# Weight conversion in pairs of tiles, with pair buffers, in a fused attention and two-layer kernel

## The chip, the cores and the metric

The kernel runs on one core of one Trainium2 chip. The metric is device time in microseconds (us) from start to end of one execution; several executions are timed and the median counts. A separate execution is taken by the hardware profiler, and its rows are what this document reads.

## What is computed

Attention with a learned relative bias, followed by two gated layers, all in fp32:

```python
scores = q @ k.T / sqrt(64) + bias(i, j)          # 4 batches, 8 heads, 576 x 576
x = softmax(scores) @ v                           # -> 2304 tokens x 512
x = (sigmoid(x @ w_gate) * (x @ w_val)) @ w_out   # 512 -> 1536 -> 512
h = x @ w_in                                      # 512 -> 2048
out = (h * clip(h + 3, 0, 6) / 6) @ w_out2        # -> 512
```

The five weight matrices come as 64-bit floats, which the host packs as they are, and are cut into 68 tiles of 128 x 512 numbers each, `wpack`, in the order of their use.

## The kernel before

**Blocks and steps.** The 576 query rows are cut into five chunks (`QC`): four of 128 and one of 64, which is 512 tokens, in the last 256, over the four batches. A *lead* stage computes the attention of chunk 0. Then come five blocks, `block(0)` to `block(4)`. Block k runs the 68 steps (`STEPS`, `NSTEP`) of the two layers on chunk k, one weight tile a step, and between the steps the attention and bias of chunk k + 1, placed by the list that `block_events` makes. So tile n mod 68 serves step n, and every tile is used five times.

**One step.** `product` multiplies with a weight tile that is split into a high half `wh` and a low half `wl`, so that fp32r matmuls (L613, L607) reach fp32: for each of four 128-row parts it runs `wh*xh`, `wh*xl`, `wl*xh`, twelve matmuls a step. In the last block the high and low half of x stand in one tile, and a step has eight or twelve shorter ones.

**The weights.** In block 0 the packed tiles are converted on the chip. `w_load` brings a raw tile `wd` (128 x 512 pairs of 32-bit words, 512 KB) from `wpack` (L531). `w_split` turns it into fp32 bits in the scratch tile `cm` and splits that: ScalarE scales the upper word (L575), VectorE shifts (L576), joins the lower word's upper bits (L577) and the sign (L580), ScalarE writes the high half (L585) and VectorE subtracts for the low half (L586). `w_store` writes the split tile `wp` to a buffer in HBM, `wsp` (L591). Blocks 1 to 4 only load split tiles from `wsp` (L535). Tiles 0 and 1 are converted in the lead by `w_part`, one operation at a time.

**Buffers and look-ahead.** There are six `wp` tiles, four raw tiles and two scratch tiles in block 0. At step n of block 0 the program issues the raw load of tile n + 6 (`WA + 1`), the store of tile n + 2 and the conversion of tile n + 3 (`WB`). From tile 68 on it issues at step n the load of tile n + 5 (`WA`).

**What sets the order.** In block 0 the instructions of TensorE and of the DMA queue SP run in the order of the program (`manual_schedule`), those of ScalarE and VectorE in an order that a planner makes at compile time. In blocks 1 to 4 only TensorE keeps the program's order; SP is planned too. Every engine then runs its instructions strictly in that fixed order. Waits come from the data: a write to a buffer waits for the last readers of the tile that had it before.

Of the kernel before, what the change touches and what calls it, by code (L numbers as in the profile page):

```python
# [30 lines left out]
SU = S + 31  # L31
WA = 5
WB = 3
# [25 lines left out]
def fused_kernel(ctx: ExitStack, tc: tile.TileContext, qd, kd, vd, tz, td, rd, zc, w2b, iden, wpack, out):  # L59
# [12 lines left out]
    z_p = pool("z", 2)  # L72
    w_p = pool("w", 6)

# [448 lines left out]

    wq, wf_q = {}, {}

    def w_load(n):
        if n >= NC * NSTEP:
            return
        if n < NSTEP:
            wd = A["wf"].tile([128, 512, 2], U32, name="wd")  # L530
            nc.sync.dma_start(out=wd.rearrange("p a b -> p (a b)"), in_=wpack[n].bitcast(U32))  # L531
            wf_q[n] = wd
        else:
            wp = w_p.tile([128, 2, 4, 128], F32R, name="wp")
            nc.sync.dma_start(out=wp.rearrange("p s c m -> p s (c m)").bitcast(F32), in_=wsp[n % NSTEP])  # L535
            wq[n] = wp

    cm_q = {}

    def w_part(n, part):  # L540

        if part == 0:
            cm_q[n] = A["cv"].tile([128, 512], U32, name="cm")
            wq[n] = w_p.tile([128, 2, 4, 128], F32R, name="wp")
        m = cm_q[n]
        f, wv = m.bitcast(F32), wq[n].rearrange("p s c m -> p s (c m)")
        low, high = wf_q[n][:, :, 0], wf_q[n][:, :, 1]
        if part == 0:
# [11 lines left out]
        elif part == 4:  # L560
            nc.vector.tensor_scalar(out=wv[:, 0], in0=f, scalar1=1.0, scalar2=None, op0=ALU.mult)
        else:
            nc.vector.tensor_tensor(out=wv[:, 1], in0=f, in1=wv[:, 0].bitcast(F32), op=ALU.subtract)
            nc.sync.dma_start(out=wsp[n], in_=wv.bitcast(F32))
            del wf_q[n], cm_q[n]

    def w_split(n):

        if n >= NSTEP:
            return  # L570
        wd = wf_q.pop(n)
        low, high = wd[:, :, 0], wd[:, :, 1]
        m = A["cv"].tile([128, 512], U32, name="cm")
        f = m.bitcast(F32)
        nc.scalar.activation(out=f, in_=high.bitcast(F32), func=AF.Copy, scale=2.0 ** -112)  # L575
# [6 lines left out]
        )  # L582
        wp = w_p.tile([128, 2, 4, 128], F32R, name="wp")
        wv = wp.rearrange("p s c m -> p s (c m)")
        nc.scalar.activation(out=wv[:, 0], in_=f, func=AF.Copy)  # L585
        nc.vector.tensor_tensor(out=wv[:, 1], in0=f, in1=wv[:, 0].bitcast(F32), op=ALU.subtract)  # L586
        wq[n] = wp

    def w_store(n):
        if 2 <= n < NSTEP:  # L590
            nc.sync.dma_start(out=wsp[n], in_=wq[n].rearrange("p s c m -> p s (c m)").bitcast(F32))  # L591

# [3 lines left out]
    def product(n, nt, ops, mm_ps, first=True, last=True, wide=False):  # L596
        wp = wq.pop(n)
        wh, wl = wp[:, 0], wp[:, 1]
        if first:
# [91 lines left out]
    with ExitStack() as lead:  # L691
        for name, bufs in (("pt", 2), ("s", 3), ("k", 6), ("v", 7), ("bo", 3), ("wf", 2), ("cv", 2)):
            A[name] = lead.enter_context(tc.tile_pool(name=name + "l", bufs=bufs))
# [63 lines left out]
    conv = ExitStack()  # L757
    for name, bufs in (("pt", 2), ("wf", 4), ("cv", 2)):
        A[name] = conv.enter_context(tc.tile_pool(name=name + "c", bufs=bufs, reuse_waits="tile"))
    ctx.enter_context(tc.issue_after(gate.ins))  # L760
    ctx.enter_context(tc.issue_after(gate_act.ins))
    for n in range(2, WA + 1):
        w_load(n)
# [133 lines left out]
    def block(k):  # L897
        ev = block_events(k)
        for i in range(NSTEP):
# [5 lines left out]
            if k == 0:  # L905
                if n + WA + 1 < NSTEP:
                    w_load(n + WA + 1)
                for x in range(WB - 1 if i == 0 else WB, WB + 1):
                    w_store(n + x - 1)
                    w_split(n + x)  # L910
            if n + WA >= NSTEP:
# [76 lines left out]
```

## Time and profile before

| what | value |
|---|---|
| three runs | 1104.69, 1105.45, 1105.76 us; median 1105.45 |
| profiled execution, its own time | 1102.25 us |
| its span, first to last instruction | 1100.2 us |
| granted TensorE clock | 1.000 of full speed (2.4 GHz) |
| lead; block 0; blocks 1 to 3; block 4 | about 0 to 84; 84 to 333; 333 to 999; 999 to 1097 us |
| busy: TensorE, VectorE, ScalarE, GpSimd | 99%, 62%, 49%, 12% of the span |

The stretches are those of the matmuls of line 613. PE is TensorE, PEld its weight load, DVE VectorE, ACT ScalarE, POOL GpSimd, SP the queue that issues most DMAs. Matmuls overlap each other and their ends are modelled. Operations of VectorE and ScalarE overlap by their ends as well, so that the distance from start to start is what one takes of the engine.

### The profile page before, as it was taken

Reading aid. Unit: us, or ns where it says so; the run is one execution under the profiler, and the core shown is the slowest. Engines: PE = TensorE matmul, PEld = TensorE weight load, DVE = VectorE, ACT = ScalarE, POOL = GpSimd, SP = SyncE. Lnnn points to the kernel's source line nnn. Section 1 sums busy time; section 2 is a strip of 40 time slices with the busy share of each in tenths; the row PEclk is TensorE's granted clock in tenths of the full one; section 3 lists DMA queues with packets and bytes.
Section 4 is the critical chain, followed back from the end, with each engine's and each line's share of the span. In section 5 each row is a group of like instructions: output and inputs, shape, how many; then the busy total and the mean of one; then the engine's idle time right before and its main releaser. Section 6 shows DMA issues by size and latency. Waiting matters only on the chain.

```text
span 1100.2 us, 19627 instructions
## 1 busy us (share of the span) xinstructions
PE 1088.0 (99%) x6964; PEld 873.7 (79%) x6964; DVE 679.8 (62%) x1571; ACT 534.7 (49%) x1087; POOL 129.9 (12%) x248
## 2 busy tenths in 40 slices
PE   8999999999999999999999999999999999999998
PEld 4777777777777787878778878788878888888898
DVE  8899998898972466887735654656352417153433
ACT  7887686798872534555424342444032214123332
POOL 2000000000010002121121111111440202031000
PEclk9999999999999999999999999999999999999999
DMA  7948999989986688999997888787996968678997
GB/s 235 369 179 296 376 396 374 387 322 370 392 291 235 212 278 288 283 318 287 308 320 249 288 248 276 263 264 248 287 289 212 286 225 280 212 242 309 370 371 272
DMA packets 118768, 321.96 MB, mean 293 GB/s; under 512 B 21008, under 2 KB 29712, under 8 KB 118672
## 3 DMA queue, kind: packets, MB, share of 16 engines
q1 hardware_dynamic: 108000, 297.15, 78.3%
q0 software_dynamic: 9152, 23.21, 7.5%
q8 instruction: 56, 0.92, 0.3%
q10 hardware_dynamic: 1520, 0.35, 0.2%
q14 instruction: 40, 0.33, 0.1%
HBM read 245.09 MB, written 51.37 MB: 269 GB/s over the span
## 4 chain that ended last, share of the span: by engine, by line
PE 82%; DVE 7%; ACT 4%; DMA 3%; issue 2%; SPq 1%; DVEq 0%; ACTq 0%
PE ps L613 61%; PE ps L430 7%; PE ps L607 6%; PE ps L477 2%; PE ps L386 2%; PE ps L335 2%; PE ps L171 1%; DVE cm L577 1%; DMA kt<-kd 1%; DVE wp L586 1%; DVE cm L580 1%; PE ps L483 1%; ACT cm L575 1%; DVE s L350 1%; DMA wd<-wpack 1%
## 5 line engine op out<-in xcount | busy, mean ns | idle before, releaser
L613 PE MATMUL ps<-xyh,wp 128*128 128x512 f32 (+1 forms) x1472 | 431.2, 379 | 0.2
L613 PEld LDWEIGHTS ps<-xyh,wp 128*128 128x128 f32 x1472 | 263.3, 188 | 58.1 <-DVE m L499 2.7
L613 PE MATMUL ps<-gh,wp 128*128 128x512 f32 (+1 forms) x980 | 298.9, 385 | 0.4 <-ACT gh L628 0.4
L613 PE MATMUL ps<-xyl,wp 128*128 128x512 f32 x640 | 249.7, 390 | 0.3 <-DVE xyl L632 0.3
L613 PEld LDWEIGHTS ps<-gh,wp 128*128 128x128 f32 x980 | 178.7, 188 | 37.7 <-issue 2.5
L613 PE MATMUL ps<-gl,wp 128*128 128x512 f32 x448 | 174.8, 390 | 0.2 <-DVE gl L630 0.2
L409 POOL DMA_DIRECT2D pT<-t x192 | 94.4, 500 | 495.1 <-DMA wp<-wsp 205.1
L628 ACT ACTIVATE gh<-tmp 128x512 fp32r<-128x512 f32 (+1 forms) x140 | 82.1, 587 | 127.5 <-DVE tmp L651 85.1
L613 PEld LDWEIGHTS ps<-xyl,wp 128*128 128x128 f32 x640 | 120.2, 188 | 24.9 <-DVE xyl L632 0.8
L360 ACT ACTIVATE s<-s,m 128x576 f32<-128x576 f32 x144 | 110.4, 769 | 23.8 <-DVE m L499 17.9
L630 DVE TENSOR_TENSOR gl<-tmp,gh 128x512 fp32r<-128x512 f32 x112 | 76.5, 685 | 35.7 <-ACT gh L628 34.8
L613 PEld LDWEIGHTS ps<-gl,wp 128*128 128x128 f32 x448 | 84.2, 188 | 17.1 <-DVE gl L630 0.7
L430 PEld LDWEIGHTS ps<-pT,vt 128*64 128x64 f32 x1600 | 79.3, 137 | 17.0 <-issue 11.6
L430 PE MATMUL ps<-pT,vt 128*64 128x128 f32 (+1 forms) x1600 | 92.1, 266 | 0.5 <-ACT pT L389 0.4
L657 DVE SCALAR_TENSOR_TENSOR tmp<-tmp,ps 128x512 f32<-128x512 f32 (+1 forms) x80 | 50.0, 628 | 55.2 <-ACT tmp L656 53.6
L651 DVE SCALAR_TENSOR_TENSOR tmp<-tmp,ps 128x512 f32<-128x512 f32 x48 | 32.7, 682 | 74.5 <-PE ps L613 73.8
L656 ACT ACTIVATE tmp<-ps 128x512 f32<-128x512 f32 (+1 forms) x80 | 43.9, 548 | 44.3 <-PE ps L613 44.0
L455 ACT ACTIVATE xyh<-ps 128x128 fp32r<-128x128 f32 (+1 forms) x52 | 16.4, 316 | 98.7 <-PE ps L430 98.5
L681 POOL DMA_DIRECT2D outT<-acc x40 | 27.7, 740 | 269.0 <-DVE acc L672 250.3
L399 DVE STREAM_TRANSPOSE t<-s 128x1152 f32<-128x1152 f32 x40 | 54.3, 1369 | 0.4
L373 DVE TENSOR_SCALAR s<-s,r 128x576 f32<-128x576 f32 x112 | 53.2, 517 | 1.4
L456 DVE TENSOR_TENSOR xyl<-ps,xyh 128x128 fp32r<-128x128 f32 (+1 forms) x48 | 16.0, 333 | 58.9 <-ACT xyh L455 58.6
(99 smaller groups left out, 1236.3 us busy)
## 6 DMA issues: line engine op xcount, KB each, us to landing
wp<-wsp SPq DMA_DIRECT2D x272, 512.0 KB, 5.1
wd<-wpack SPq DMA_DIRECT2D x68, 512.0 KB, 6.4
wsp<-wp SPq DMA_DIRECT2D x68, 512.0 KB, 6.0
vt<-vd SPq DMA_DIRECT2D x80, 320.0 KB, 5.0
kt<-kd SPq DMA_DIRECT2D x80, 288.0 KB, 5.3
pT<-t POOLq DMA_DIRECT2D x192, 72.0 KB, 4.9
pT<-t SPq DMA_DIRECT2D x128, 72.0 KB, 4.5
bm<-biasD SPq DMA_DIRECT2D x15, 576.0 KB, 6.4
```

What stands on the lines that cost most here:

```text
L360: nc.scalar.activation(out=s[:, h], in_=s[:, h], func=AF.Exp, scale=-1.0, bias=d["m"][:, h:h + 1], accum_out=r[:, h:h + 1],)
L373: nc.vector.tensor_scalar(out=s[:, h], in0=s[:, h], scalar1=r[:, h:h + 1], scalar2=None, op0=ALU.mult)
L399: nc.vector.transpose(out=tn_q[0][:, :, x], in_=st[u]["s"].rearrange("p h j -> p (h j)").rearrange("p (t q j) -> p q t j", q=4, j=32),)
L409: (nc.sync if p[0][0] < 4 and i > 1 else nc.gpsimd).dma_start(out=pt[32 * q:32 * q + 32, i].rearrange("j u t i -> j (u t i)"), in_=t[32 * ...
L430: nc.tensor.matmul(out=po[64 * h:64 * h + 64, n * a:n * a + n], lhsT=vt[:, v], rhs=pt[:, m * a:m * a + m, k, :], start=(t == 0), stop=(t = ...
L607: nc.tensor.matmul(out=o, lhsT=w[:, c, :], rhs=x, start=(first and c == 0 and w is wh), stop=(last and c == 3 and w is wh),)
L613: nc.tensor.matmul(out=ps[:, 0:nt], lhsT=w[:, c, :], rhs=x[:, 0:nt], start=(first and c == 0 and i == 0), stop=(last and c == 3 and i == 2),)
L628: nc.scalar.activation(out=hi, in_=src, func=AF.Copy, scale=scale)
L630: nc.vector.tensor_tensor(out=lo, in0=src, in1=hi.bitcast(F32), op=ALU.subtract)
L651: nc.vector.scalar_tensor_tensor(out=th, in0=th, scalar=1.0, in1=ps, op0=ALU.add, op1=ALU.mult)
L656: nc.scalar.activation(out=t, in_=ps, func=AF.Relu, bias=3.0)
L657: nc.vector.scalar_tensor_tensor(out=t, in0=t, scalar=6.0, in1=ps, op0=ALU.min, op1=ALU.mult)
```

## The change

Raw tiles, scratch and split tiles become pairs: `wp` has three buffers of two tiles each (the same memory as six), the raw tiles in block 0 three buffers of two (six tiles for four). From tile 4 on `w_split` runs each of its six operations once over two tiles, called at every second step for tiles n + 3 and n + 4; tiles 2 and 3 are done singly at step 0. The raw load of tile n + 7 (`WR`) is issued at step n, the store of tile n + 1 (for n + 2 before), and from tile 68 on the load of tile n + 4 (for n + 5). The scratch no longer has a pool of its own in block 0: up to tile 17 it takes a buffer of `pT`, then one of `z`.

```diff
--- before.py
+++ after.py
@@ -29,7 +29,8 @@
 NT = 320
 SW = S + NQ - 1
 SU = S + 31
-WA = 5
+WA = 4
+WR = 7
 WB = 3
 YG, OG = 3, 2
 BIG = 3.0e38
@@ -70,7 +71,7 @@
     st_p = pool("st", 4)
     bm_p = pool("bm", 2)
     z_p = pool("z", 2)
-    w_p = pool("w", 6)
+    w_p = pool("w", 3)
 
 
     s1 = pool("ps_s", 2, space=PS)
@@ -521,19 +522,28 @@
         att_x(p[0], po)
         del st[p[1]]
 
-    wq, wf_q = {}, {}
+    wq, wf_q, wp_q = {}, {}, {}
+
+    def w_tiles(n, k=1):
+
+        if n % 2 == 0:
+            wp_q[0] = w_p.tile([128, 2, 2, 512], F32R, name="wp")
+        for x in range(k):
+            wq[n + x] = wp_q[0][:, (n + x) % 2]
+        return wp_q[0][:, n % 2:n % 2 + k]
 
     def w_load(n):
         if n >= NC * NSTEP:
             return
         if n < NSTEP:
-            wd = A["wf"].tile([128, 512, 2], U32, name="wd")
-            nc.sync.dma_start(out=wd.rearrange("p a b -> p (a b)"), in_=wpack[n].bitcast(U32))
-            wf_q[n] = wd
+            if n % 2 == 0:
+                wf_q[0] = A["wf"].tile([128, 2, 512, 2], U32, name="wd")
+            nc.sync.dma_start(
+                out=wf_q[0][:, n % 2].rearrange("p a b -> p (a b)"), in_=wpack[n].bitcast(U32)
+            )
+            wf_q[1, n] = wf_q[0][:, n % 2:2]
         else:
-            wp = w_p.tile([128, 2, 4, 128], F32R, name="wp")
-            nc.sync.dma_start(out=wp.rearrange("p s c m -> p s (c m)").bitcast(F32), in_=wsp[n % NSTEP])
-            wq[n] = wp
+            nc.sync.dma_start(out=w_tiles(n)[:, 0].bitcast(F32), in_=wsp[n % NSTEP])
 
     cm_q = {}
 
@@ -541,10 +551,10 @@
 
         if part == 0:
             cm_q[n] = A["cv"].tile([128, 512], U32, name="cm")
-            wq[n] = w_p.tile([128, 2, 4, 128], F32R, name="wp")
+            w_tiles(n)
         m = cm_q[n]
-        f, wv = m.bitcast(F32), wq[n].rearrange("p s c m -> p s (c m)")
-        low, high = wf_q[n][:, :, 0], wf_q[n][:, :, 1]
+        f, wv, wd = m.bitcast(F32), wq[n], wf_q[1, n][:, 0]
+        low, high = wd[:, :, 0], wd[:, :, 1]
         if part == 0:
             nc.vector.tensor_scalar(out=f, in0=high.bitcast(F32), scalar1=2.0 ** -112, scalar2=None, op0=ALU.mult)
         elif part == 1:
@@ -562,16 +572,20 @@
         else:
             nc.vector.tensor_tensor(out=wv[:, 1], in0=f, in1=wv[:, 0].bitcast(F32), op=ALU.subtract)
             nc.sync.dma_start(out=wsp[n], in_=wv.bitcast(F32))
-            del wf_q[n], cm_q[n]
-
-    def w_split(n):
+            del cm_q[n]
+
+    def w_split(n, k=2):
 
         if n >= NSTEP:
             return
-        wd = wf_q.pop(n)
-        low, high = wd[:, :, 0], wd[:, :, 1]
-        m = A["cv"].tile([128, 512], U32, name="cm")
-        f = m.bitcast(F32)
+        wd = wf_q[1, n][:, 0:k]
+        low, high = wd[:, :, :, 0], wd[:, :, :, 1]
+        if n < 18:
+            m = A["pt"].tile([128, 9, NQ], F32, name="pT").rearrange("p t n -> p (t n)")
+        else:
+            m = z_p.tile([128, 4, S], F32, name="z").rearrange("p g j -> p (g j)")
+        f = m[:, 0:512 * k].rearrange("p (s a) -> p s a", s=k)
+        m = f.bitcast(U32)
         nc.scalar.activation(out=f, in_=high.bitcast(F32), func=AF.Copy, scale=2.0 ** -112)
         nc.vector.tensor_scalar(out=m, in0=m, scalar1=3, scalar2=None, op0=ALU.logical_shift_left)
         nc.vector.scalar_tensor_tensor(
@@ -580,22 +594,20 @@
         nc.vector.scalar_tensor_tensor(
             out=m, in0=high, scalar=0x80000000, in1=m, op0=ALU.bitwise_and, op1=ALU.bitwise_or
         )
-        wp = w_p.tile([128, 2, 4, 128], F32R, name="wp")
-        wv = wp.rearrange("p s c m -> p s (c m)")
-        nc.scalar.activation(out=wv[:, 0], in_=f, func=AF.Copy)
-        nc.vector.tensor_tensor(out=wv[:, 1], in0=f, in1=wv[:, 0].bitcast(F32), op=ALU.subtract)
-        wq[n] = wp
+        wv = w_tiles(n, k)
+        nc.scalar.activation(out=wv[:, :, 0], in_=f, func=AF.Copy)
+        nc.vector.tensor_tensor(out=wv[:, :, 1], in0=f, in1=wv[:, :, 0].bitcast(F32), op=ALU.subtract)
 
     def w_store(n):
         if 2 <= n < NSTEP:
-            nc.sync.dma_start(out=wsp[n], in_=wq[n].rearrange("p s c m -> p s (c m)").bitcast(F32))
+            nc.sync.dma_start(out=wsp[n], in_=wq[n].bitcast(F32))
 
 
     ys, gs, accs, th_q, ps_q = {}, {}, {}, {}, {}
 
     def product(n, nt, ops, mm_ps, first=True, last=True, wide=False):
         wp = wq.pop(n)
-        wh, wl = wp[:, 0], wp[:, 1]
+        wh, wl = (wp[:, s].rearrange("p (c m) -> p c m", c=4) for s in range(2))
         if first:
             ps_q[0] = mm_ps()
         ps = ps_q[0]
@@ -689,7 +701,7 @@
     NL = len(us)
     NG0, NG1 = QC[0][1] // 16, 2
     with ExitStack() as lead:
-        for name, bufs in (("pt", 2), ("s", 3), ("k", 6), ("v", 7), ("bo", 3), ("wf", 2), ("cv", 2)):
+        for name, bufs in (("pt", 2), ("s", 3), ("k", 6), ("v", 7), ("bo", 3), ("wf", 1), ("cv", 2)):
             A[name] = lead.enter_context(tc.tile_pool(name=name + "l", bufs=bufs))
         lead.enter_context(tc.manual_schedule(engines={ET.PE, ET.Activation, ET.DVE, ET.SP}))
         load_rows(us[0], False)
@@ -755,11 +767,11 @@
     P = dict(gu=late("gu", 12), tmp=late("tmp", 3), acc=late("acc", 4))
     A.update(k=late("k", 4), v=late("v", 4), s=late("s", 2))
     conv = ExitStack()
-    for name, bufs in (("pt", 2), ("wf", 4), ("cv", 2)):
+    for name, bufs in (("pt", 2), ("wf", 3)):
         A[name] = conv.enter_context(tc.tile_pool(name=name + "c", bufs=bufs, reuse_waits="tile"))
     ctx.enter_context(tc.issue_after(gate.ins))
     ctx.enter_context(tc.issue_after(gate_act.ins))
-    for n in range(2, WA + 1):
+    for n in range(2, WR):
         w_load(n)
 
     def chunk_bias(c, t0, dt, done=0):
@@ -903,11 +915,14 @@
                 held.extend((issued[1], issued[2]))
             n = k * NSTEP + i
             if k == 0:
-                if n + WA + 1 < NSTEP:
-                    w_load(n + WA + 1)
-                for x in range(WB - 1 if i == 0 else WB, WB + 1):
-                    w_store(n + x - 1)
-                    w_split(n + x)
+                if i == 0:
+                    w_split(2, 1)
+                    w_split(3, 1)
+                if n + WR < NSTEP:
+                    w_load(n + WR)
+                w_store(n + 1)
+                if i % 2:
+                    w_split(n + WB)
             if n + WA >= NSTEP:
                 w_load(n + WA)
             moe_step(k, i, P, mm_ps)
```

## Rows read from the trace of the kernel before

**Rows 1.** The page, part 1: busy time, share of span, instructions

```profile
PE 1088.0 (99%) x6964; PEld 873.7 (79%) x6964; DVE 679.8 (62%) x1571; ACT 534.7 (49%) x1087; POOL 129.9 (12%) x248
```

**Rows 2.** Table by stretch: length, PE, PEld, DVE, ACT, POOL, clock, DMA share, GB/s

```profile
132.00:150.00 18.00, 18.00 (x87) 13.44 (x86) 17.43 (x39) 14.60 (x29) 0.00 (x0) 1.00 1.03 416
...
168.00:333.00 165.00, 164.62 (x1007) 129.14 (x1005) 141.66 (x302) 130.74 (x264) 4.18 (x6) 1.00 0.96 353
...
999.00:1097.00 98.00, 97.21 (x640) 88.85 (x639) 40.83 (x98) 37.55 (x97) 1.37 (x2) 1.00 0.93 345
```

**Rows 3.** Waits of PE, 84 to 1097 us: total, times, longest (first row)

```profile
PE ps L430 <- ACT pT L389: 0.4, 1, 0.4
```

**Rows 4.** DVE in time (start, length), two stretches; and page group of L399

```profile
133.86 0.42 DVE L576 TENSOR_SCALAR cm<-cm 128x512 uint32<-128x512 uint32 x1
134.20 0.68 DVE L586 TENSOR_TENSOR wp<-cm,wp 128x512 fp32r<-128x512 f32 x1
134.80 0.68 DVE L577 SCALAR_TENSOR_TENSOR cm<-wd,cm 128x512 uint32<-128x512 uint32 x1
...
445.31 2.63 DVE L399 STREAM_TRANSPOSE t<-s 128x1152 f32<-128x1152 f32 x2
...
L399 DVE STREAM_TRANSPOSE t<-s 128x1152 f32<-128x1152 f32 x40 | 54.3, 1369 | 0.4
```

**Rows 5.** PE in order of time, 142 to 152 us

```profile
146.75 0.48 PE L613 MATMUL ps<-xyh,wp 128*128 128x512 f32 x1
...
147.46 0.74 PE L613 MATMUL ps<-xyh,wp 128*128 128x512 f32 x2
```

**Rows 6.** DVE in order of time, 141 to 152 us

```profile
146.72 0.69 DVE L586 TENSOR_TENSOR wp<-cm,wp 128x512 fp32r<-128x512 f32 x1
...
150.19 0.69 DVE L586 TENSOR_TENSOR wp<-cm,wp 128x512 fp32r<-128x512 f32 x1
```

**Rows 7.** Stretches from 0, of L613 (PE) and of L586 (DVE): count in brackets

```profile
0.00:146.74 146.74, 56.80 (x240) 1.00 0.82 299
...
0.00:150.20 150.20, 12.94 (x20) 1.00 0.83 301
```

**Rows 8.** Waits of the weight load, 142 to 152 us

```profile
PEld ps L613 <- DVE wp L586: 0.9, 2, 0.5
```

**Rows 9.** Waits of DVE, 88 to 151 us

```profile
DVE cm L576 <- ACT cm L575: 2.6, 4, 1.3
```

**Rows 10.** ACT in order of time, 126 to 131 us; in brackets idle time before

```profile
129.97 0.68 ACT L575 ACTIVATE cm<-wd 128x512 f32<-128x512 f32 x1 [0.90 <-DMA wd<-wpack]
```

**Rows 11.** Line 535 in narrow stretches: length, first and last start; time to landing

```profile
L535 SPq DMA_DIRECT2D wp<-wsp x1: 332/332/332, 862.6 to 862.6; - x1
...
DMA to landing us min/median/max: 12.4/12.4/12.4
...
L535 SPq DMA_DIRECT2D wp<-wsp x1: 320/320/320, 865.2 to 865.2; - x1
...
DMA to landing us min/median/max: 12.9/12.9/12.9
...
L535 SPq DMA_DIRECT2D wp<-wsp x1: 320/320/320, 878.8 to 878.8; - x1
...
DMA to landing us min/median/max: 3.2/4.8/5.3
...
L535 SPq DMA_DIRECT2D wp<-wsp x1: 320/320/320, 1018.2 to 1018.2; - x1
...
DMA to landing us min/median/max: 6.4/6.4/6.4
...
L535 SPq DMA_DIRECT2D wp<-wsp x1: 319/319/319, 1025.2 to 1025.2; - x1
```

**Rows 12.** SP in order of time, 849 to 882 us

```profile
856.30 2.57 SPq L297 DMA_DIRECT2D kt<-kd  x4
858.92 0.59 SPq L289 DMA_DIRECT2D qt<-qd  x1
```

## The prediction

> **What bounds the kernel now.** I read the page's busy line first. TensorE is busy 1088.0 of the span's 1100.2 us, so only some 12 us of the span lack a matmul [rows 1]. A busy TensorE need not be at its peak, so the second view is the table by stretch. In block 0, from 168 to 333 us, TensorE lacks 0.4 us of 165, and in the last block 0.8 us of 98 [rows 2]. The waits say the same: four entries between 84 and 1097 us, the largest 0.4 us [rows 3]. So nearly everything outside TensorE is hidden. The change can win only what TensorE still waits for, and it loses whatever it makes TensorE wait for.
>
> The third question is how near each feeder is to being late. Two are, and the change touches both.
>
> The first is VectorE in block 0. It converts 66 of the 68 weight tiles there (tiles 2 to 67) and is busy 17.43 of 18 us between 132 and 150 us, with the DMA engines full as well (share 1.03) [rows 2]. Conversion is just in time there. Step 20 has its first matmul at 146.75; the third is the first to read the low half, which the subtraction of L586 writes at 146.72 + 0.69 = 147.41, and it starts at 147.46 [rows 5, 6]. The counts name the tile: 240 product matmuls (20 steps of 12) lie ahead of 146.74, and the L586 at 150.19 is the 20th, which is tile 21 as the first is tile 2 [rows 7]. The weight loads waited 0.9 us in these steps for the two L586 [rows 8]. Matmuls follow each other every 0.23 us or so, and about 0.4 of the 0.9 is real delay by my estimate.
>
> The second is the stream of converted tiles from `wsp` later on. In block 3 a load issued at 865.2 lands 12.9 us later, at 878.1. Loads are issued as TensorE gives buffers back, five steps ahead, so the load five places on, at 878.8, marks the step that needs it: 0.7 us of slack. In block 4 the load of 1018.2 lands at 1024.6 and is needed at 1025.2: 0.6 us [rows 11].
>
> **The change part by part.**
>
> *Operations over two tiles.* Tiles 4 to 67 become 32 pairs; four VectorE and two ScalarE operations per pair replace eight and four. What one merge saves is read from start to start, since operations overlap. Of 512 elements, L586 is followed 0.60 us later and L576 0.34 us later; two L399 of 1152 elements take 2.63 us, and one lasts 1.37, so the second starts 2.63 - 1.37 = 1.26 us after the first [rows 4]. The slope is (1.26 - 0.60)/640 = 1.03 ns an element. A 1024-element operation should thus take 0.60 + 0.53 = 1.13 against 1.20, and the shift, which runs at double rate, 0.34 + 0.26 = 0.60 against 0.68. That is 3 x 0.07 + 0.08 = 0.29 us a pair, 9.3 us of VectorE over block 0. None of this is on the path of a full TensorE: the direct gain is zero, but it pays for the next item.
>
> *A pair is ready only as a whole.* The even tile now waits for the odd one. The tightest pair I found is (20, 21): tile 21 was done at 150.88 and must now be done by 147.46, 3.4 us earlier [rows 5, 6]. By then 9 pairs have saved 9 x 0.29 = 2.6 us, which leaves 0.8. VectorE also stood idle 2.6 us between 88 and 151 us ahead of L576, waiting for ScalarE's first pass [rows 9], which in turn waited for a raw tile [rows 10]. So the ends are: 3.4 us of stall if nothing is regained, 0.8 if the savings accumulate and no idle time goes, and a gain of 0.4 if both work. I take 0.3, because the idle time has causes that the next item removes.
>
> *Raw loads seven ahead, six raw tiles instead of four.* A load waits for the tile that had its buffer six tiles ago, no longer four; that is two steps, some 6 us, earlier than now, against a raw-tile wait of 0.9 us [rows 10]. A pair needs both raw halves, the second of which is a step younger, so one of the two steps remains. The DMA engines are full in this stretch, so this moves loads into the emptier start and adds no rate. Cost nothing; if the loads kept their place the pair would start one load later, and that is inside the 3.4.
>
> *Tiles 2 and 3 singly, scratch in the buffers of `pT` or `z`.* The first two tiles convert as now. There are two scratch buffers, as now, each twice as long. `z` is used by block 0's bias work up to step 9 and `pT` by attention from step 18, and the scratch uses each outside that time. Nothing queues behind it. Zero, from 0 to one operation of 1.13 us.
>
> *Store one step later; queue SP.* Behind a store or raw load that waits for a conversion stand the next store and attention's k and v loads. Those k loads are issued two units ahead, and SP is released by the same conversions as now. TensorE never waited for a DMA from 84 us on [rows 3]. Zero. Longer VectorE operations can hold an eviction up by 0.53 us each; TensorE has four banks to go on with, and no wait for one is seen. Zero, at most 0.5.
>
> *Three pair buffers and weights four steps ahead.* A pair buffer comes free when both tiles are used. The odd tile's load keeps its place, since its half is free as soon as the even one's is; the even tile's is issued one step later, 2.7 us in block 3 and 1.4 in block 4. That the halves of one buffer count apart is seen in step 20, which began on the high half at 146.75 while the low half was written until 147.41 [rows 5, 6]. At both tight places a queue hides the later issue. The step is 13.6/5 and 7.0/5 us by the loads five places apart. In block 3 the load of 862.6 lands at 875.0, so the one of 865.2 could not move before about then; issued 2.7 later it is still 7 us before its turn. In block 4 a load lands 3.2 us after issue at best, and the one of 1018.2 took 6.4, so 3.2 us of it were queue, more than the 1.4 that it loses [rows 11]. Zero if loads land in queue order. If every load, the odd ones too, moves one place down the queue, slack falls by a step: 0.7 - 2.7 = -2.0 and 0.6 - 1.4 = -0.8. Ends 0 and 2.8; I take zero, because the planner orders SP by readiness: k loads went out at 856.30 before the q load of 858.92 that the program issues ahead of them [rows 12], so an odd load that is ready should follow its even one at once.
>
> *Sum.* 0.3 + 0 = +0.3 us on the profiled execution's 1102.25, and the median of the runs is 1105.45, 3.2 above it. Forecast 1105.8, no change that can be seen.
>
> One rule differs from the rows in price. The Trainium skill, "VectorE: DVE Perf Modes", section "The TRN2 errata", gives a measured fixed term of about 150 cycles at 0.96 GHz per operation, which would be an estimated 0.62 us a pair and 5.6 us by pair (20, 21), so that there would be no stall at all. The start-to-start rows [rows 4] say half of it, and the sum goes by them.
>
> **The rivals.**
>
> *The pair comes late (slower).* VectorE is busy 97% of 132 to 150 us; other work stands between a pair's operations, which now block it for 1.13 us. If the static order gives the pairs no better place, TensorE stalls 3.4 us at step 20, less the 0.4 that it has now: 1105.45 + 3.0 = 1108.5. It decides as soon as tile 21's low half is later than step 20's third matmul by 2 us or more. For it: tight by 3.4. Against it: 2.6 + 2.6 us of slack. The Trainium skill speaks for this one: "Perfetto Trace Analysis", section "Optimizing Scalar/DVE Operations", says that breaking up instructions may let work finish sooner where the engine causes bubbles on others, and this change does the reverse.
>
> *The queue slips a place (slower).* As priced: 2.0 + 0.8 = 2.8, 1108.3. It decides if the planner leaves odd loads at their place in the program, behind a burst of k, v and bias loads. Against it: the order of [rows 12].
>
> *A wider gain (faster).* All that TensorE lacks goes: 0.4 in the just-in-time conversion, 0.4 in the rest of block 0, 0.8 in the last block, and the other three entries of the waits at up to 0.4 each, 2.8 us at most: 1102.7. Nothing in the change reaches the last block's share, so this is unlikely.
>
> **How the numbers follow.** Forecast 0.66, own range 1104.7 to 1107.2; late pair 0.15; slipped queue 0.13; wider gain 0.06. Both slow cases together give 1111.3 and are rare. The range 1104.0 to 1109.5 leaves out about 2 in 10. About 0.2%, 2.2 us, is what a measurement tells from no change. Slower by more: both slow cases less the part of them that ends small, 0.27; faster by more, 0.05; the rest 0.68.
>
> **What would show it.** L577 at 128x1024 some 32 times with about 1.2 us each, and VectorE's sum in block 0 down by about 9 us; right if TensorE still lacks about 0.4 us between 168 and 333 us and next to nothing more from 84 to 168. Late pairs would show as TensorE waits for L586 between 109 and 150 us. A slipped queue would show as waits for `wp<-wsp` near 870 and 1024 us. The forecast is wrong if a wait of over 1 us appears anywhere in these stretches, or if planned engines take another order elsewhere.

## The result and the profile after

The changed kernel takes 1113.7 us (median of four runs, 1112.32 to 1116.62) against 1105.07 us for the kernel before, run beside it on the same chip. The ratio is 1.0092, with a 95% interval of 1.0078 to 1.0106. It is 8.6 us slower, and outside the range of 1104.0 to 1109.5. The profiled execution took 1113.18 us with a span of 1111.4 us, 11.2 longer than that of before.

Busy time of each engine in the changed kernel (page, part 1), to set beside [rows 1]:

```profile
PE 1094.3 (98%) x6964; PEld 876.4 (79%) x6964; DVE 670.3 (60%) x1443; ACT 526.6 (47%) x1023; POOL 129.9 (12%) x248
```

VectorE lost 9.5 us of work (679.8 before), as priced: 9.3. Both kernels' table by stretch shows what became of it (length, busy PE, PEld, DVE, ACT, POOL, then granted clock, DMA share, GB/s). First the kernel before, for the stretch of 84 to 168 us, which [rows 2] doesn't have; then the changed kernel.

```profile
84.00:168.00 84.00, 83.78 (x436) 63.78 (x436) 78.13 (x152) 62.09 (x114) 2.13 (x4) 1.00 0.96 358
```

```profile
84.00:168.00 84.00, 80.94 (x407) 61.06 (x404) 70.37 (x99) 55.31 (x85) 2.13 (x4) 0.98 0.90 327
...
132.00:150.00 18.00, 15.93 (x66) 11.00 (x64) 15.53 (x22) 10.70 (x17) 0.00 (x0) 0.91 1.03 407
168.00:333.00 165.00, 162.19 (x991) 126.17 (x990) 139.22 (x227) 128.72 (x229) 2.20 (x4) 0.99 0.94 340
999.00:1108.00 109.00, 108.47 (x758) 98.29 (x756) 41.96 (x100) 37.72 (x98) 5.47 (x8) 1.00 0.93 342
```

TensorE now lacks 2.07 us between 132 and 150 us, and in the same 18 us VectorE is idle for 2.5 where it had been idle for 0.6 [rows 2]. VectorE idles in the very stretch in which TensorE waits, so it is not short of capacity there. The waits of TensorE from 84 us on (total, times, longest), against [rows 3]:

```profile
PE ps L625 <- DVE wp L599: 3.2, 3, 1.8
PE ps L625 <- ACT wp L598: 2.2, 2, 1.5
PE ps L625 <- ACT gh L640: 0.9, 1, 0.9
```

L599 is the low half (L586 before), L598 the high half (L585), L625 the product (L613). Five waits for converted tiles hold 5.4 us. In order of time (start, length, in brackets the wait ahead of the matmul):

```profile
99.23 0.73 PE L625 MATMUL ps<-xyh,wp 128*128 128x512 f32 x2 [0.85 <-DVE wp L599]
...
143.62 0.50 PE L625 MATMUL ps<-xyh,wp 128*128 128x512 f32 x1 [1.54 <-ACT wp L598]
144.88 0.86 PE L625 MATMUL ps<-xyh,wp 128*128 128x512 f32 x2 [0.53 <-DVE wp L599]
...
169.33 0.50 PE L625 MATMUL ps<-gh,wp 128*128 128x512 f32 x1 [0.67 <-ACT wp L598]
...
171.89 0.73 PE L625 MATMUL ps<-gh,wp 128*128 128x512 f32 x2 [1.83 <-DVE wp L599]
```

They belong to pairs (4,5), (18,19) and (24,25). Behind the waits for the last two pairs the clock drops. The table by stretch, for (24,25):

```profile
172.00:176.00 4.00, 4.00 (x12) 2.70 (x14) 2.39 (x3) 1.50 (x2) 0.00 (x0) 0.58 1.07 365
176.00:180.00 4.00, 4.00 (x37) 3.14 (x38) 2.40 (x5) 1.04 (x3) 0.00 (x0) 1.00 0.94 347
```

The granted clock is 0.58 and then 1.00 of full speed, that is for most of the first stretch at the lower level, 1.2 of 2.4 GHz; product matmuls follow each other every 0.43 us there instead of every 0.23. This costs about 1.7 us (0.42 of 4 us): step 24 to step 26 grew by 3.65 us, of which 1.83 was the wait.

The best account of where the time went is when each step of block 0 starts (its first product matmul; twelve to a step), in microseconds after the same step of the kernel before, each in its profiled execution. Labels are those of the experiments.

| step | changed | e1 | h2 | e4 | f3 | h3 | g2 | h1 | g1 |
|---|---|---|---|---|---|---|---|---|---|
| 0 | 1.1 | 0.6 | 0.6 | 0.6 | 1.3 | 0.5 | 0.0 | -0.3 | -0.2 |
| 6 | 2.3 | 0.6 | 0.6 | 0.6 | 2.5 | 1.7 | 0.0 | -0.3 | -0.2 |
| 16 | 2.3 | 0.6 | 0.6 | 0.6 | 2.5 | 4.5 | 0.0 | -0.2 | -0.2 |
| 20 | 6.8 | 5.9 | 0.6 | 2.4 | 4.3 | 8.0 | 0.6 | 3.5 | -0.2 |
| 26 | 10.6 | 5.3 | -0.1 | 2.1 | 8.0 | 10.4 | -0.1 | 2.9 | -0.9 |
| 68 | 10.7 | 6.3 | 0.0 | 3.6 | 7.9 | 16.8 | -0.6 | 3.7 | -2.1 |
| last matmul | 11.3 | 6.8 | 1.7 | 4.6 | 10.8 | 19.5 | -0.5 | 3.8 | -1.9 |

In the changed kernel 1.15 us come at steps 4 to 6, 4.5 at steps 16 to 20, 3.9 at steps 20 to 26, and 0.6 in blocks 1 to 4. The 1.1 at step 0 I do not count as part of the change: f1, which alters nothing ahead of block 0, starts its step 0 2.6 us late in its profiled execution, and the runs that share all that the change does ahead of it start it between 0.2 us early (h4) and 1.3 late (e3).

### The profile page after: what moved, and what is told of

Read it like the earlier page. It is cut to its first block, busy times and chain, and to the rows that moved or that the text cites. A ratio compares the mean times of both kernels' runs of the same rounds, so it can differ in the third digit from the quotient of the medians.

```text
span 1111.4 us, 19156 instructions
## 1 busy us (share of the span) xinstructions
PE 1094.3 (98%) x6964; PEld 876.4 (79%) x6964; DVE 670.3 (60%) x1443; ACT 526.6 (47%) x1023; POOL 129.9 (12%) x248
## 4 chain that ended last, share of the span: by engine, by line
PE 79%; DVE 9%; DMA 5%; ACT 3%; issue 2%; SPq 0%; DVEq 0%; ACTq 0%
PE ps L625 58%; PE ps L431 7%; PE ps L619 6%; PE ps L478 3%; DMA wd<-wpack 2%; PE ps L387 2%; PE ps L336 2%; DVE wp L599 2%; DVE z L591 1%; DMA wsp<-wp 1%; PE ps L172 1%; DVE z L594 1%; DVE s L351 1%; DVE gl L642 1%; PE ps L484 1%
## 5 line engine op out<-in xcount | busy, mean ns | idle before, releaser
L625 PE MATMUL ps<-xyh,wp 128*128 128x512 f32 (+1 forms) x1472 | 432.8, 380 | 3.0 <-ACT wp L598 1.5
L625 PEld LDWEIGHTS ps<-xyh,wp 128*128 128x128 f32 x1472 | 263.9, 189 | 61.9 <-issue 3.4
L625 PE MATMUL ps<-gh,wp 128*128 128x512 f32 (+1 forms) x980 | 300.2, 386 | 3.4 <-DVE wp L599 1.8
L625 PE MATMUL ps<-xyl,wp 128*128 128x512 f32 x640 | 250.6, 392 | 0.4 <-DVE xyl L644 0.3
L625 PEld LDWEIGHTS ps<-gh,wp 128*128 128x128 f32 x980 | 179.2, 189 | 41.9 <-issue 2.5
L625 PE MATMUL ps<-gl,wp 128*128 128x512 f32 x448 | 175.3, 391 | 0.2 <-DVE gl L642 0.2
L625 PEld LDWEIGHTS ps<-xyl,wp 128*128 128x128 f32 x640 | 120.6, 188 | 25.1 <-DVE xyl L644 1.0
L625 PEld LDWEIGHTS ps<-gl,wp 128*128 128x128 f32 x448 | 84.5, 189 | 17.1 <-DVE gl L642 0.7
L659 ACT ACTIVATE tmp<-ps 128x512 f32<-128x512 f32 x48 | 28.5, 594 | 48.8 <-PE ps L625 48.5
```

Source lines behind the costliest of these rows:

```text
L625: nc.tensor.matmul(out=ps[:, 0:nt], lhsT=w[:, c, :], rhs=x[:, 0:nt], start=(first and c == 0 and i == 0), stop=(last and c == 3 and i == 2),)
```

## The mechanism in the trace: a pair's chain is longer than a tile's

Take the earliest loss, pair (4,5), where nothing has slipped yet but the first 84 us. VectorE in order of time, kernel before (tiles 4 and 5, scratch `cm`), then the changed kernel (pairs (4,5) and (6,7), scratch `pT`):

```profile
89.30 0.43 DVE L576 TENSOR_SCALAR cm<-cm 128x512 uint32<-128x512 uint32 x1
89.76 0.69 DVE L577 SCALAR_TENSOR_TENSOR cm<-wd,cm 128x512 uint32<-128x512 uint32 x1
90.37 0.42 DVE L576 TENSOR_SCALAR cm<-cm 128x512 uint32<-128x512 uint32 x1
...
93.11 0.68 DVE L586 TENSOR_TENSOR wp<-cm,wp 128x512 fp32r<-128x512 f32 x1
...
94.31 0.68 DVE L586 TENSOR_TENSOR wp<-cm,wp 128x512 fp32r<-128x512 f32 x1
```

```profile
90.87 0.69 DVE L590 TENSOR_SCALAR pT<-pT 128x1024 uint32<-128x1024 uint32 x1 [0.60 <-ACT pT L589]
91.60 1.23 DVE L591 SCALAR_TENSOR_TENSOR pT<-wd,pT 128x1024 uint32<-128x1024 uint32 x1
92.74 0.69 DVE L590 TENSOR_SCALAR pT<-pT 128x1024 uint32<-128x1024 uint32 x1
93.34 0.68 DVE L663 SCALAR_TENSOR_TENSOR tmp<-tmp,ps 128x512 f32<-128x512 f32 x1
93.94 1.22 DVE L594 SCALAR_TENSOR_TENSOR pT<-wd,pT 128x1024 uint32<-128x1024 uint32 x1
95.08 1.22 DVE L591 SCALAR_TENSOR_TENSOR pT<-wd,pT 128x1024 uint32<-128x1024 uint32 x1
96.21 0.69 DVE L642 TENSOR_TENSOR gl<-tmp,gh 128x512 fp32r<-128x512 f32 x1
96.81 1.22 DVE L594 SCALAR_TENSOR_TENSOR pT<-wd,pT 128x1024 uint32<-128x1024 uint32 x1
97.95 1.22 DVE L599 TENSOR_TENSOR wp<-pT,wp 128x1024 fp32r<-128x1024 f32 x1
```

In both kernels two units are in hand, one in each scratch buffer, and the order takes their operations in turn. A unit's *chain* is the time from the start of its first pass on ScalarE to the end of its low half. Before, the unit is a tile, and the chain of tile 4 took 5.2 us (88.59 to 93.79). Now the unit is a pair, and (4,5) took 9.5 us (89.70 to 99.17), since operations of twice the length of pair (6,7), at 92.74, 95.08 and 96.81, stand between its own. Before, tile 4 was done 3.3 us ahead of its third matmul, the first to read the low half (97.06). 5.2 us of chain that become 9.5 take 4.3 us, which makes it 1.0 us late; the wait at 99.23 is 0.85 from the modelled end of the matmul before it, and step 6 starts 1.15 us later. Over tiles 4 to 33 a chain took 5.9 us on average before, and over the same pairs 9.5 us (7.2 to 13.5). That accounts for the first of the three losses. For the other two it is also the start of the chain that counts, as e3 shows below.

## The experiments

Times are medians beside a run of the kernel before in the same session (1103.75, 1103.59, 1103.84, 1103.42 and 1103.28 us for the labels with e, f, g, h and i).

**One tile an operation (e1) and pairs later on (e2).** Everything else is as in the change.

```
-                if i % 2:
-                    w_split(n + WB)
+                if i:
+                    w_split(n + WB, 1)
```

> All of the change stays (pair buffers, raw loads seven ahead, scratch in pT and z, weights four ahead later), but every operation of the conversion works on one tile again. Whole-pair theory (a tile waits for its partner through six long operations): TensorE no longer waits over 0.5 us for a weight in block 0, 1105 to 1106.5 us. Raw-queue theory (a raw pair buffer comes free only when both halves are converted, so raw tiles land late behind a full DMA queue): waits between 130 and 175 us stay, 1109 to 1113. Other parts (scratch, four steps ahead): as the changed kernel, 1112 to 1115.

Measured: 1110.03 us, ratio 1.0047 [1.0026, 1.0069]. The waits for tiles 4 and 24 are gone, as whole pairs would have it; one at steps 16 to 18 stays, with operations over single tiles. So there were two causes. The second, as it shows with single tiles, is in VectorE's order (L590 shift, L599 low half; tile 17 in `pT`, tile 18 in `z`), with TensorE's wait behind it:

```profile
130.77 0.43 DVE L590 TENSOR_SCALAR z<-z 128x512 uint32<-128x512 uint32 x1 [0.47 <-ACT z L589]
...
132.50 0.42 DVE L590 TENSOR_SCALAR pT<-pT 128x512 uint32<-128x512 uint32 x1
...
139.94 0.68 DVE L599 TENSOR_TENSOR wp<-z,wp 128x512 fp32r<-128x512 f32 x1
140.55 0.69 DVE L599 TENSOR_TENSOR wp<-pT,wp 128x512 fp32r<-128x512 f32 x1
...
141.29 0.73 PE L625 MATMUL ps<-xyh,wp 128*128 128x512 f32 x2 [2.37 <-DVE wp L599]
```

Tile 18 starts ahead of tile 17 and is done ahead of it, while TensorE waits for tile 17. Where the scratch changes from `pT` to `z`, four buffers can be in use, so nothing holds tile 18 back.

e2 takes single tiles up to tile 27 and pairs from there (`if 0 < i < 25: w_split(n + WB, 1)`, then as in the change).

> Tiles 2 to 27 are converted singly, tiles 28 to 67 in pairs, all else as in the change. If only the stretch up to step 27 is tight, both the whole-pair and the raw-queue theory expect 1105 to 1106.5 us and no wait over 0.5 us for a weight. If pairs also cost something where there is slack (longer operations in front of attention and evictions), 1107 or more with waits after 180 us.

Measured: 1108.73 us, 1.0046 [1.0028, 1.0065]; the same wait at step 17 (2.37 us), and nothing more from the pairs after tile 28. Pairs cost only where converted tiles are tight.

**Fewer stores (e3).** Tiles 8 to 27 are not stored, and tiles 28 to 47 are loaded in their place in blocks 1 to 4.

> The changed kernel without the stores of tiles 8 to 27 (10 MB less to write between about 105 and 180 us); blocks 1 to 4 load tiles 28 to 47 in their place, so the weights of those steps are other ones and the traffic there is the same. Raw-queue theory: raw tiles land in 6 to 7 us where they took 9.5 to 10.5, and TensorE's waits for weights between 130 and 175 us fall from 5.5 us to under 1.5, about 1105 to 1107 us; the first one, near 99 us, stays. Whole-pair theory: pairs stay late, waits of 4 us or more remain, 1109 or more.

Measured: 1110.53 us in a single execution. The waits at steps 16 to 26 are gone (2.5 us behind at step 6, 1.85 at step 26), but later steps lose nearly as much: 5.15 us behind at step 68, 8.7 at the end. Why they do was not followed.

The run shows that a long chain by itself does not make pairs (18,19) and (24,25) late. ScalarE's first passes over these two, in the changed kernel and then in e3:

```profile
135.39 1.14 ACT L589 ACTIVATE z<-wd 128x1024 f32<-128x1024 f32 x1
...
158.38 1.12 ACT L589 ACTIVATE z<-wd 128x1024 f32<-128x1024 f32 x1
```

```profile
125.20 1.15 ACT L589 ACTIVATE z<-wd 128x1024 f32<-128x1024 f32 x1 [0.95 <-DMA wd<-wpack]
...
146.85 1.14 ACT L589 ACTIVATE z<-wd 128x1024 f32<-128x1024 f32 x1
```

Over tiles 4 to 33 the chains of e3 are even longer, 11.2 us on average against 9.5. But these two pairs start 10.2 and 11.5 us sooner, and are done 3.4 and 7.8 us ahead of their third matmuls. The wait for (4,5) stays (0.83 us). Raw tile 17 was issued at 114.24 us and landed at 122.03, against 119.04 and 129.44 in the changed kernel, where VectorE then stood idle for 5.1 us between 114 and 132 us (0.8 in e3, 2.2 before). So the waits for (18,19) and (24,25) need a late start beside the long chain. Whether the stores make the start late by their traffic or by their place in SP's order, this run doesn't separate.

**Last two operations by tile (e4, and again as g3; g4).** The pair's high and low halves are written tile by tile, the even one first, in place of the two operations over the pair:

```
+        for x in range(k):
+            nc.scalar.activation(out=wv[:, x, 0], in_=f[:, x], func=AF.Copy)
+            nc.vector.tensor_tensor(out=wv[:, x, 1], in0=f[:, x], in1=wv[:, x, 0].bitcast(F32), op=ALU.subtract)
```

> The changed kernel, with the last two operations (high half on ScalarE, low half on VectorE) done per tile, the even one first; the first four stay over two tiles. The even tile is then ready some 1.7 us earlier (a 1.13 us subtraction less 0.6, and one high half of about 0.5 to 1.0 less) and the odd one as before. Whole-pair theory: waits of 0.9, 1.5, 0.5, 0.7 and 1.8 us all shrink, to 1 to 2 us in sum, 1106 to 1108 us. Raw-queue theory: the pairs start as late as before; the same 1.7 us is gained at each wait, but pairs that start after 129 us stay late by the rest, 1108 to 1111.

> The changed kernel with its last two operations for each tile by itself, the even tile first, as in e4_last_two_singly, timed in rounds. By the theory that the late even tile and the operations between made the waits at tiles 4, 18 and 24: they are gone, block 0 loses at most 2.5 us against before (the first 84 us apart), 1105 to 1108.5 us. If the one look was a chance: 1110 to 1114.

Measured: e4 1106.56 us in a single execution, g3 1107.18 us, 1.0035 [1.0022, 1.0049]. Two operations more for each pair, and 5 to 6 us less than the change. The waits for tiles 4, 18 and 24 are gone; one of 1.2 us for the high half of tile 20 is left, and what else it loses are in the main single waits for ScalarE of up to 1.9 us. The Trainium skill, "Perfetto Trace Analysis", section "Optimizing Scalar/DVE Operations", says that breaking up instructions may let work complete sooner where ScalarE or VectorE isn't saturated but causes bubbles on other engines. This run agrees: 1.0035 against 1.0092, and in the changed kernel VectorE was busy for 15.5 of the 18 us from 132 to 150 us while TensorE waited for it.

g4 adds the scratch in `z` from tile 14 on.

> The run with the last two operations for each tile by itself, with scratch from z from tile 14 on instead of tile 18. Pairs keep two scratch tiles, so four tiles, in hand at all times; where the switch stands should then matter less than with single operations: between the time of the run beside it and 2 us less, as the 1.8 us that it still loses at steps 18 to 20 go: 1104 to 1108 us. If the switch makes a new wait at tiles 12 to 15 as it did with single operations: 3 to 5 us more than the run beside it.

Measured: 1107.59 us, 1.0032 [1.0019, 1.0045], the same as g3. Written like this, where the scratch changes matters little.

**The scratch: alone (f1), and its change moved (f2, f3).** f1 is the kernel before with the scratch of the change. f2 is e1, and f3 the changed kernel, with `if n < 14` in place of `if n < 18`.

> The kernel before with one part of the change alone: the conversion's scratch lies in the buffers of pT up to tile 17 and of z from tile 18, instead of two buffers of its own. Raw tiles (four, five ahead), converted tiles, operations over one tile and stores are those of before. Theory of the scratch: tiles 18 and 19 no longer wait for the scratch of 16 and 17, so four tiles are in hand at once, the planner takes their operations in turn and tile 17 gets its low half late: a TensorE wait of 2 to 2.5 us for it in steps 16 to 18, a stretch of lower clock behind it, 4 to 6 us more, 1108 to 1110 us. Theory of the raw tiles (pair buffers or loads seven ahead make raw tiles late at steps 16 to 18): nothing here, 1104 to 1105.5 us, no wait over 0.9 us.

> The run with one tile an operation (e1_singles) again, with scratch from z from tile 14 on instead of tile 18. Theory of the scratch: the turn with four tiles in hand moves from tiles 16 to 19 to tiles 12 to 15; the wait of 2.4 us at steps 16 to 18 goes, and comes back smaller or not at all at steps 12 to 14, where VectorE has more idle time: 1104.5 to 1107 us. Theory of the raw tiles: the wait at steps 16 to 18 stays, about 1110 us.

> The changed kernel with scratch from z from tile 14 on instead of tile 18, nothing else. If whole pairs cost by themselves, the waits for tiles 4 and 24 (0.8 and 2.5 us) stay and only that for tiles 18 and 19 (2.1 us with the clock behind it) goes or shrinks: 1108 to 1111 us. If the switch of the scratch made all of the loss, some 1105.5 us.

Measured: f1 1102.6 us, 0.9993 [0.9983, 1.0002], and none of TensorE's listed waits from 84 us on is for a conversion. f2 1113.42 us, 1.0084 [1.0055, 1.0113]: the wait left steps 16 to 18 and came back at step 13, the last tile in `pT`, and no smaller (2.97 us for its high half, in an execution of 1108.46 us, one of the fastest). f3 1113.25 us, 1.0083 [1.0067, 1.01]: steps 16 to 20 lose 1.8 us instead of 4.5, steps 20 to 26 still 3.7, and blocks 1 to 4 lost 2.9 more, so the total is hardly better. Taken together, the change of the scratch is the place of the second cause with single tiles, but by itself it costs nothing. In the changed kernel moving it takes 2.7 us off steps 16 to 20; how much of the wait for (18,19) is due to it is not shown beyond that.

**Weights four ahead (f4).** The kernel before with converted tiles in three pair buffers and `WA = 4`.

> The kernel before with converted tiles in three buffers of two tiles and weights loaded four steps ahead in blocks 1 to 4; raw tiles, scratch, operations and stores as before. As predicted this part costs nothing: 1104 to 1105.5 us, and the steps of blocks 1 to 4 keep their time within 0.5 us. By the rival of the slipped queue: 2.8 us more, with waits for weight loads near 870 and 1024 us.

Measured: 1104.95 us, 1.0021 [1.0006, 1.0037]. The two longest of its waits from 84 us on:

```profile
PE ps L617 <- ACT gh L632: 1.2, 1, 1.2
PE ps L617 <- DVE wp L591: 0.4, 1, 0.4
```

Waits for `wp<-wsp` sum to 0.2 us, so the slipped queue didn't come. It costs some 2 us all the same: in the profile blocks 1 to 4 lose 1.8 us, where I had expected under 0.5, and 0.8 of it is a longer wait for `gh`, an operand of the layer that ScalarE writes (1.2 us, 0.4 before). The same matmul of block 1 waits 0.9 us in the changed kernel, and 0.4 in g1, g2, h1 and i1, which keep the weights of before. What made it late was not followed.

**Raw loads earlier: alone (g1, i2) and with the scratch (g2).** g1 is the kernel before with five single raw tiles loaded six ahead; i2 is g1 again. g2 has six raw tiles, seven ahead, and the scratch of the change.

```
-    for name, bufs in (("pt", 2), ("wf", 4), ("cv", 2)):
+    for name, bufs in (("pt", 2), ("wf", 5), ("cv", 2)):
```

> The kernel before with raw loads earlier as the one part: five single raw tiles loaded up to six ahead instead of four loaded five ahead; scratch, converted tiles, operations and stores as before (six raw tiles and a scratch of its own would not fit). If earlier loads alone make the wait at steps 16 to 18: a TensorE wait of over 1 us there and 1107 to 1110 us. If it takes both, loads that let four tiles be in hand and a scratch that gives room for them, nothing here: 1102.5 to 1105 us, no wait for a converted tile over 0.5 us.

> The kernel before with five raw tiles instead of four, loaded up to six ahead, once more and in more rounds (g1_five_raw gave a ratio of 0.9959). If the gain is real: 0.994 to 0.998 of before. If it was the spread of the first 84 us from run to run: 0.999 to 1.001.

> The kernel before with the two parts together: six single raw tiles loaded seven ahead, and scratch in the buffers of pT up to tile 17 and of z from tile 18; converted tiles in six single buffers, weights five ahead later, operations over one tile and stores as before. By the theory of both together: the turn with four tiles in hand at tiles 16 to 19 as in the run with single operations in pair buffers, a wait of 2 to 3 us for tile 17, then a stretch of lower clock, 4 to 5 us more at step 20 against step 16: 1107 to 1110 us. If it were the buffers of two raw tiles that cost there: no wait, 1103 to 1105 us.

Measured: g1 1100.15 us, 0.9959 [0.9934, 0.9984]; i2 1101.13 us, 0.9971 [0.9956, 0.9986]; g2 1101.97 us, 0.9983 [0.9974, 0.9993]. So raw loads alone make the kernel 2 to 4 us faster than before, which I had not expected. All waits of g1 from 84 us on:

```profile
PE ps L614 <- ACT gh L629: 0.4, 1, 0.4
PE ps L614 <- DVE xyl L633: 0.3, 1, 0.3
PE ps L614 <- DVE gl L631: 0.2, 1, 0.2
```

None is for a converted tile; the 0.7 us gained at steps 20 to 22 are what tiles 20 and 21 had lost before (0.9 us of waiting in the weight load [rows 8]). And g2 fails the theory that earlier loads and the scratch together make the second cause: it has both and no wait over 0.4 us.

**The stores: one step later (h1, i1), and back (h2, h3, h4).** h1 is g2 with the store of the change, i1 the kernel before with it. h2 is e1, h3 the changed kernel and h4 is g3, each with the store of before, as here in h3:

```
-                w_store(n + 1)
+                w_store(n + 2)
```

> The run before with six raw tiles and the shared scratch (g2_six_raw_and_scratch, no wait there), with one thing added: each tile's store stands one step later in SP's order, as in the change. Theory of the store: stores stood in front of raw loads and kept the plan from taking up tiles 18 and 19 before 16 and 17 were done; one step later they let it, VectorE's operations of four tiles are taken in turn at the switch of the scratch, and tiles 16 to 18 are late: a wait of 1.5 to 3 us at steps 16 to 18, 3 to 5 us more from step 16 to step 20, 1106 to 1109 us. Theory of the pair buffers: no wait there, 1101.5 to 1103.5 us.

> The kernel before with one thing changed: each tile's store stands one step later in SP's order. Four raw tiles, scratch of its own in two buffers. If the late store only costs where the scratch changes from pT to z and gives room for four tiles in hand: no wait over 0.6 us at steps 16 to 20, 1102 to 1105 us. If the late store costs by itself: a wait of over 1 us there, 1106 us or more.

> The run with one tile an operation in pair buffers (e1_singles, 2.4 us of waiting at tile 17), with the stores back at their place of before, one step earlier. Theory of the store: VectorE takes tiles 16 to 19 in the order of the run with six single raw tiles, the wait goes, block 0 loses at most 1 us: 1102.5 to 1105.5 us. Theory of the pair buffers: the wait stays, 1108 to 1111 us.

> The changed kernel with one thing undone: stores one step earlier, as before. Theory: the part of the loss at tiles 18 and 19 (4.4 us from step 16 to 20) goes or shrinks to under 2 us, what whole pairs cost at tiles 4 and 24 (1.1 and 3.6 us) stays: 1107 to 1110.5 us. If the store has no part in it where operations take pairs: 1112 to 1114.

> The changed kernel with both undone: stores one step earlier, and the last two operations for each tile by itself. By the two causes together all of the loss of block 0 but the lead's goes: 1103.5 to 1106.5 us, no wait for a converted tile over 0.6 us. Anything over 1108 says that a third cause is left in block 0.

Measured: h1 1106.68 us, 1.0039 [1.0024, 1.0054], where g2 had 0.9983, with waits of 1.7 and 1.2 us at steps 16 and 17. i1 1103.99 us, 1.0000 [0.9981, 1.0018], with one wait of 0.5 us for a converted tile, at step 18. h2 1103.66 us, 1.0009 [0.9993, 1.0025], where e1 had 1.0047. The waits of h1 for converted tiles:

```profile
PE ps L618 <- DVE wp L591: 1.7, 1, 1.7
PE ps L618 <- ACT wp L590: 1.2, 1, 1.2
```

VectorE in h2, against the rows of e1:

```profile
131.48 0.42 DVE L590 TENSOR_SCALAR pT<-pT 128x512 uint32<-128x512 uint32 x1
131.84 0.43 DVE L590 TENSOR_SCALAR z<-z 128x512 uint32<-128x512 uint32 x1
...
136.73 0.68 DVE L599 TENSOR_TENSOR wp<-pT,wp 128x512 fp32r<-128x512 f32 x1
...
139.29 0.68 DVE L599 TENSOR_TENSOR wp<-z,wp 128x512 fp32r<-128x512 f32 x1
```

Tile 17 now goes first and is done 3.8 us sooner. So the second cause is the late store together with the change of the scratch, shown over six raw tiles and with operations over one tile: the store alone (i1), the scratch alone (f1), and the scratch with six raw tiles (g2) cost nothing. Pair buffers have no part in it, since h1 has none and waits, and h2 has them and doesn't. Not tried was the late store with the new scratch over four raw tiles, nor six raw tiles with a scratch of their own, which doesn't fit the memory. Why a store's place in SP's order turns VectorE's order round is the planner's doing, and was not followed further.

With whole pairs it is the other way round: h3 took 1121.54 us, 1.0169 [1.0142, 1.0196], 8 us worse than the change, and h4 1108.41 us, 1.0047 [1.0032, 1.0062], no better than g3. Both miss what I expected. SP's longest group of waits between 84 and 180 us, first in the changed kernel, then in h3:

```profile
SPq L603 <- DVE wp L599: 23.2, 9, 4.8
```

```profile
SPq L603 <- DVE wp L599: 43.7, 10, 6.8
```

The store of an even tile now waits for the whole pair, and the raw loads stand behind it on SP. One step earlier it waits longer, while the raw loads' own waits shrink from 24 us to 1, so that SP waits about as long in all. The raw loads go out later for it: tile 17 was issued at 125.69 us and landed at 132.63 (119.04 and 129.44 in the changed kernel), and TensorE waited 2.3 us for pair (16,17) at step 16. h3 loses another 6.4 us at steps 26 to 68 and 2.7 in blocks 1 to 4, which were not followed. So with whole pairs an earlier store does harm, and with single tiles and this scratch a later one does. The two causes do not simply add up: with the store back, nothing comes off the change (h3), nor off g3 (h4).

## Why the prediction was wrong

- *Operations over two tiles.* Right. The low half over 1024 elements lasts 1.22 us and is followed after 1.13 (97.95 to 99.08), the shift after 0.60 (160.30 to 160.90). VectorE's 9.5 us saved are 0.30 us a pair against 0.29. The fixed term of the Trainium skill ("VectorE: DVE Perf Modes", "The TRN2 errata"), by my estimate 0.62 a pair, is not what VectorE gets back here. It shows in the length of an operation (two of 0.68 become one of 1.22, 0.14 less), but only half of that in the distance from start to start (two of 0.60 become 1.13 or 1.14).
- *A pair is ready only as a whole.* This step failed, at +0.3 us where about 5 to 6 were lost (the change against g3). I moved the deadline of one pair, (20,21), and let VectorE's savings over all earlier pairs pay for it. Left out was how long one unit is on its way. With two units taken in turn, doubling the operations took a chain from 5.9 to 9.5 us on average. The pair I had chosen wasn't even late: it ended at 152.80, in time for a step that had slipped by then. The late ones were (4,5), (18,19) and (24,25): the first by its chain alone, the other two by their chains and a late start (e3). Work saved on an engine does not buy back the length of a chain: VectorE's busy time in 84 to 168 us fell by 7.8 us while TensorE waited for it (by my estimate some 3 of them were savings, 10 pairs of 0.30; the rest was work that the later kernel had not reached).
- *Tiles 2 and 3 singly, scratch*, and *store one step later*. Each was priced at zero, and alone each is (f1, i1). Together, over six raw tiles and with single tiles, they cost 4 to 6 us (h1 against g2, e1 against h2); in the changed kernel their share stays open. I had checked what queues behind a store, not that a plan made anew would let tile 18 pass tile 17.
- *Raw loads seven ahead.* Priced at nothing. It gains 0.3 to 0.4% alone, six ahead (i2, g1), and 0.2% with the scratch (g2). In the changed kernel it did not bring the raw tiles one step, some 3 us, sooner where the big loss begins: tiles 16 and 17 were issued at 114.65 and 119.04 and landed at 121.46 and 129.44; before they landed at 127.27 and 129.89. A pair needs the later one, and the first pass of (16,17) began at 129.54.
- *Three pair buffers and weights four ahead.* Nearly zero in the changed kernel: blocks 1 to 4 lose 0.6 us, 0.5 of it in the longer wait for `gh`. Alone 0.2% (f4), inside its two ends of 0 and 2.8, but without the weight waits that the upper end stood for.
- *The rivals.* "The pair comes late" was the right mechanism with the wrong place and price: 3.0 us at step 20, against three places, 0.9 us of stall at the first and 2.1 and 2.5 at the others, with the clock falling behind them. "The queue slips a place" and the wider gain did not come.

What I would have needed was in the trace of before: the first pass and low half of tile 4, 88.59 to 93.79, and its third matmul 3.3 us later. Doubling the chain there gives a late pair at once. The two larger losses it would not have priced.

## What to carry to other kernels

Before merging operations over two units, price the chain of one unit and not only the engine's sum: with several units taken in turn, each one's time on its way grows with the length of the operations (here 1.6 times on average for operations over two units), and it is compared with the smallest margin of the *first* unit of each pair. When a unit can start is a term beside it. Edits that each cost nothing can cost together where a planner writes the order anew, so the likely order where a buffer changes is a term of its own. And take the parts apart: the one that was thought a supplement, raw tiles loaded earlier, is worth 0.3 to 0.4% by itself.

## What the runs showed of the hardware

- A stall of TensorE can cost nearly twice. Behind the waits of 1.54 and 0.53 us at 143 to 145 us the granted clock was 0.83, 0.50 and 0.82 of full speed in the three stretches of 2 us from 144 on; behind those of 0.67 and 1.83 us at 169 to 172 us it was 0.58 from 172 to 176. Each time another 1.7 us went. It isn't so behind every wait: h1 waited 1.68 and 1.20 us within 4 us, and its clock stayed at 1.00 from 132 to 150 us. Which decides was not found.
- With the DMA engines full (share 1.03 between 132 and 150 us in both kernels), a load that is issued earlier need not land as much earlier. Raw tiles issued between 119 and 138 us took 9.4 to 10.5 us to land in the changed kernel, and 6.7 to 8.7 before; tile 17 was issued 2.5 us sooner than before and landed 0.5 sooner. In e3, with twenty stores less and a share of 0.77, they took 5.5 to 8.1 us.
